# The last matrix products of a fused retention and maxout kernel: two chains change places, and one tile's product is taken by seven products

## The chip, the cores and the metric

The kernel runs on one core of a Trainium2 chip. A core has five engines that work side by side, each on its own queue of instructions in order: TensorE (PE, matrix products into PSUM), VectorE (DVE), ScalarE (ACT), GpSimd (POOL) and SyncE (SP, which here issues the loads and stores). The metric is the device time of one execution in microseconds, the median of several runs.

## The reference

Retention attention gives `x`, and a maxout feed-forward layer with three input matrices and one output matrix follows:

```python
scores = scale * q @ k.T                       # B, H, S, D = 8, 8, 576, 64
ret = scores * where(i >= j, gamma[h] ** (i - j), 0)
x = (ret @ v)                                  # as (4608, 512)
h = maximum(maximum(x @ w1, x @ w2), x @ w3)   # w1..w3: (512, 768)
out = h @ w_out                                # w_out: (768, 512)
```

All is in float32. The weights come as 64-bit floats and are converted in the kernel.

## The kernel before, in words

The 4608 rows are worked in nine tiles of 512 rows (`NT`). For each tile `ffn(t)` computes `h`, held transposed as 6 blocks of 128 features by 512 rows (`h[:, fb, :]`), in three pairs of blocks `fp`, taken in the order 0, 2, 1. Then it multiplies by `w_out`. While a tile runs, the attention of the next tile is put between its products (`steps`, `values`, `scores`).

The first tile's products are plain: `up_plain` and `downs_plain`. From the second tile (`t == 1`) the products of `up` follow a fast scheme with 20 products per block pair (`PRODUCTS`) in chains A to E, each chain a bank in PSUM into which products are added; ACT copies partial sums out (L718, `part`) and DVE joins them (L721). The second tile's down-projection is still `downs_plain` (L745): 6 blocks of `h` times 4 row blocks of 128, 24 matmuls of 512 columns, summed in four banks, then four ACT copies (L749) and four outputs. From the third tile on, `downs` runs 20 products (`DOWNS`, L578), each of two matmuls with 256 columns, in chains C to I. "Place" below is the position in `DOWNS`; `TOTALS` says what is read out after which place, by ACT copy (L567) or DVE sum (L484). The left operands such as `n8` or `b41` are sums of parts of `h` (`HIDDEN_SUMS`), the right ones such as `v13` are sums of parts of `w_out` (`OUT_SUMS`). Two chains share one bank: E with G, H with D, F with C. I has one of its own:

```python
        for pool, tag, chains in ((ps_y, "y", "EG"), (ps_y, "y", "I"), (ps_x, "x", "HD"), (ps_x, "x", "FC")):
...
            begins = chain in "IHEFD" and chain not in begun
```

The pools `ps_x` and `ps_y` have two banks each, handed out in turn, so the next tile's first B chain takes the bank that held H, its first A the bank that held F, its first E the one of E and G. In the profile these banks are called `deg`, `di`, `dhd` and `dfc`; matmuls of `downs` carry their name.

The order on each engine is the order in which the program issues. DVE work that isn't urgent waits in two lists, `urgent` and `chores`; `chore(n)` issues up to `n` of them, and is called between products: after each product of `downs` twice, then one `vraw` scaling on ACT (`scale`, L204). So DVE's queue mixes the totals with the next tile's sums of `x` (`s19`, `s15`, ... L484), transposes (`kT`, `qT`, L209) and masks (L330). `keep_chunk` puts factors on POOL (L340). SP issues loads and outputs in order. Each matmul of float32 appears in the profile as two instructions. `late_room` holds the tiles `late["V"]` and `late["N"]`, which the third tile fills; in the second tile they are not used yet.

Of the kernel before, what the change touches and what calls it, by code (L numbers as in the profile page):

```python
# [40 lines left out]
FP32 = mybir.dt.float32  # L41
# [4 lines left out]
ALU = mybir.AluOpType  # L46
PSUM = bass.MemoryType.PSUM

C = 128
NT = 4 * C  # L50
NH = NT // 2
# [11 lines left out]
            b23 = b43 - b23, n7 = b42 + n4, n5 = b22 + b23, b43 = b41 - b43, b41 = b41 - n5, b23 = b32 + b23,  # L63
            b21 = b21 - b41, b42 = b42 - n5, b22 = b22 - b21, n6 = b31 + n2, b32 = b22 - b32, n8 = b12 - n4,
            b31 = b31 + b32"""
# [15 lines left out]
OUT_SUMS = """m14 = -c21 - c23, m6 = m14 - c13, v19 = c11 - m6, v15 = c12 + v19, v22 = c22 + v15, v3 = v15 + m14,  # L81
              m7 = -c13 - c23, m11 = m7 - c22, v13 = c12 - m11, v10 = c11 + v13, c23 = c22 + c23"""

DOWNS = """I b13 c13, H n1 m14, E b12 c12, H n5 v15, F n7 c22, G n8 c22, E b11 c11, I n2 m6, H b41 v19, I b43 m7,
           H b42 c12, I n4 m11, G n3 c21, I b33 c23, D n6 c21, I b32 v10, C b22 v13, I b23 v3, C b31 c11, I b21 v22"""

TOTALS = {1: "k1 = I", 2: "k14 = H", 4: "k15 = H", 7: "y11 = E + k1", 8: "k6 = I", 9: "k19 = H", 10: "k7 = I",
          11: "y14 = H - k6, k19 = k19 - k6", 12: "k11 = I, k14 = k11 - k14, y24 = F + k14", 13: "y21 = G - k11",
          14: "k20 = I", 15: "y23 = D + k20", 16: "k10 = I, k1 = k1 + k10", 17: "u = C + k7, u = u + k19",
          18: "k3 = I, y12 = u - k3", 19: "k7 = C + k7, y13 = k7 - k1", 20: "y22 = I - k15"}  # L90
X_SUMS, W_SUMS = ([x.split() for x in text.split(",")] for text in (X_SUMS, W_SUMS))
PRODUCTS, DOWNS, OUT_SUMS = ([x.split() for x in text.split(",")] for text in (PRODUCTS, DOWNS, OUT_SUMS))
# [6 lines left out]
def kernel(  # L99
# [14 lines left out]
    nc = tc.nc  # L114
    P = 128
# [29 lines left out]
    def half(j):  # L145
        return slice(D * j, D * (j + 1))
# [55 lines left out]
    def scale(n=1):  # L202
        for _ in range(min(n, len(scaling))):
            scaling.popleft()()  # L204

    def chore(n=1):
        for _ in range(n):
            if urgent or chores:
                (urgent or chores).popleft()()  # L209
# [177 lines left out]
    def head(c, n):  # L387

        return NP * c + n
# [90 lines left out]
            for n, line in enumerate(X_SUMS):  # L480
                soon(partial(step, n, *line))

    def combine(dst, a, b, sign):
        nc.vector.tensor_tensor(dst, a, b, op=ALU.add if sign == "+" else ALU.subtract)  # L484

# [14 lines left out]
    def load_weights(n):  # L502
        for _ in range(n):
            if not to_load:
                return
            i, fb = piece = to_load.popleft()
            if fb % 2 == 0:
                bits[i, fb // 2] = wraw.tile([P, 2, DM], I64, tag="bits", name="bits")
            t = bits[i, fb // 2][:, fb % 2, :]
            if i == "out":  # L510
                nc.sync.dma_start(t, moe_w_out[fb * P:(fb + 1) * P, :])
            else:
                heads = WS[i][:, fb * P:(fb + 1) * P].rearrange("(h p) f -> p h f", p=D)
                blocks = t.rearrange("p (n f) -> p n f", f=P)
                for c in range(2):
                    nc.sync.dma_start(blocks[half(c)], heads[:, head(c, 0):head(c, NP)])

    def groups(order):

# [27 lines left out]
    def downs(t, h, order):  # L547
        n8, n23, n6 = (ppool.tile([P, m, 2, P], FP32, tag="part", name="n") for m in (1, 2, 1))
        late_ones = {"n8": n8[:, 0], "n2": n23[:, 0], "n3": n23[:, 1], "n6": n6[:, 0]}
        for step in sums_of_hidden(h, order, 1, late_ones):  # L550
            step()
        banks = {}
        for pool, tag, chains in ((ps_y, "y", "EG"), (ps_y, "y", "I"), (ps_x, "x", "HD"), (ps_x, "x", "FC")):
            b = pool.tile([P, 2, DM // 2], FP32, tag=tag, name="d" + chains.lower())
            banks.update({chain: b[:, n] for n, chain in enumerate(chains)})
        begun, parts = set(), {}

        def total(dst, _, a, sign=None, b=None):
            a, b = (banks.get(x, parts.get(x)) for x in (a, b))
            if dst[0] == "y":  # L560
                place = opool.tile([P, DM // 2], FP32, tag="osb", name="osb")[:]
            else:
                if dst not in parts:
                    parts[dst] = ppool.tile([P, DM // 2], FP32, tag="part", name=dst)[:]
                place = parts[dst]
            if sign is None:
                nc.scalar.copy(place, a)  # L567
            else:
                combine(place, a, b, sign)
            if dst[0] == "y":  # L570
                i, j = int(dst[1]) - 1, int(dst[2]) - 1
                nc.sync.dma_start(out[t * NT + j * P:t * NT + (j + 1) * P, i * DM // 2:(i + 1) * DM // 2], place)

        for n, (chain, b, v) in enumerate(DOWNS):
            begins = chain in "IHEFD" and chain not in begun
            begun.add(chain)
            for e in range(2):
                nc.tensor.matmul(banks[chain], lhsT=hidden(h, order, b, late_ones)[:, e], rhs=late["V"][v][:, e],  # L578
                                 start=begins and e == 0, stop=chain not in [x[0] for x in DOWNS[n + 1:]] and e == 1,
                                 skip_group_check=True)  # L580
            for line in TOTALS.get(n + 1, ()):
                total(*line)
            yield
# [100 lines left out]
    def weight_sums(fp):  # L684

        def step(dst, a, sign, b):
            combine(*(factor(n, slice(2 * fp, 2 * fp + 2)) for n in (dst, a, b)), sign)

        for dst, _, a, sign, b in W_SUMS:
            chores.append(partial(step, dst, a, sign, b))  # L690
        chores.append(partial(summed_fp.add, fp))
# [98 lines left out]
    def ffn(t):  # L790

        h = hpool.tile([P, NF, NT], FP32, tag="h", name="h")
        if t == 0:
            for fp, i in units:
                if (fp, i) == units[0]:
                    first_ups(h)
                    yield
                    continue
                for fb in (2 * fp, 2 * fp + 1):
                    maximum, = up_plain(t, h, fb, i)  # L800
                    if (fp, i) == units[-1] and fb % 2:
                        maximum()
                        convert(2)
                    else:
                        convert(4 if (fp, i) == units[1] else 2)
                        maximum()
                    if (fp, i, fb) == (*units[1], 0):
                        scores(CPT)
                        state(CPT)
                        keep(CPT)  # L810
                yield
            convert(3)
            for fb, _ in enumerate(downs_plain(t, h, range(NF // 2))):
                convert(2 if fb < 2 else 4 * len(pieces))
                if fb == 2:
                    while_converting.close()
                    late["pool"] = ctx.enter_context(tc.tile_pool(name="late", bufs=1))
                    state_factors()
                    nc.gpsimd.tensor_copy(causal[half(1), 0:D], causal[half(1), half(1)])
                    late_room()  # L820
                    weight_sums(0)
                elif fb == 3:
                    chore(len(chores))
                if fb in (1, 3):
                    yield
            yield
            return
        order = (0, 2, 1)
        if t == 1:
            spread.append(True)  # L830
            weight_sums(2)
            weight_sums(1)
        if t == 2:
            out_sums(order)
        total = len(order) * 2 * len(PRODUCTS)
        count = parts = 0
        for fp in order:
            while fp not in summed_fp:
                chore()
            for step, _ in enumerate(up(t, h, fp)):  # L840
                if step % 4 == 1 or step % 4 == 3 and len(urgent) > (2 if t == 1 else 6):
                    chore(len(urgent) > 0)
                elif chores:
                    chores.popleft()()
                if step % 3 == 2:
                    scale()
                count += 1
                if count * (NF // 2 * 3) >= (parts + 1) * total:
                    parts += 1
                    yield  # L850
            if t > 1 and fp != order[-1]:
                chores.extend(sums_of_hidden(h, order, 3 - order.index(fp)))
        chore(len(urgent) + len(chores))
        if t == 1:
            for n, _ in enumerate(downs_plain(t, h, order)):
                chore(5)
                scale(3)
                if n in (1, 3):
                    yield
        else:  # L860
            for n, _ in enumerate(downs(t, h, order)):
                chore(2)
                scale()
                if n in (3, 9):
                    yield
        yield
# [146 lines left out]
```

## Time and profile before

| | |
|---|---|
| median of 3 runs | 751.48 us (750.33 to 751.66) |
| the profiled execution | 751.75 us, span 749.9 us |
| PE busy | 739.0 us (99%), 6680 instructions |
| DVE busy | 569.6 us (76%), 1040 instructions |
| ACT, POOL busy | 336.2 us (45%), 28.3 us (4%) |
| matmuls of `downs_plain`, L745 | 96 instructions, 42.1 us busy (two tiles) |
| granted clock of PE | 0.999 of full speed |

In the profile a line such as `L745 PE MATMUL down<-w_out,h` is a group: code line, engine, operation, what is written and what is read. In a timeline the first two numbers are the start and the time taken, in us from the span's start, and brackets tell how long the engine stood idle and what released it. PEld is the loading of a matmul's stationary operand, which overlaps other matmuls. Starts are measured; the ends of matmuls are modelled.

### The profile page before, as it was taken

To read this page: it belongs to the slowest core of one execution; us is meant where nothing else is said; L and a number is where in the kernel's file an instruction comes from. 1 tells how busy PE (TensorE), PEld (TensorE's weight loads), DVE (VectorE), ACT (ScalarE), POOL (GpSimd) and SP (SyncE) were. 2 spreads that over 40 slices of the span, in tenths; PEclk is the share of its full clock that TensorE was granted. 3 is DMA by queue.
4 is the path that set the end of the run, shared out by engine and by line. 5 is a ranking of instruction groups with operands and counts; after the bars stand their busy time and mean duration, and the time that the engine had idled before them with its cause. 6 is when DMAs were issued, how large, how long until landed. Compare 5 with 4: busy or idle time off the path is not lost.

```text
span 749.9 us, 16732 instructions
## 1 busy us (share of the span) xinstructions
PE 739.0 (99%) x6680; PEld 600.7 (80%) x6680; DVE 569.6 (76%) x1040; ACT 336.2 (45%) x693; POOL 28.3 (4%) x36
## 2 busy tenths in 40 slices
PE   8999999999999999999999999999999999999998
PEld 6645546887588888888888888888888888888886
DVE  3988899987576895689668876688668956893675
ACT  3764533454245433644254435542455245424441
POOL 2000000001000100000000001000100010000000
PEclk9999999999999999999999999999999999999999
DMA  9996842504152515142433243232514151000001
GB/s 208 239 247 142 225 93 75 96 15 91 47 98 43 98 32 111 38 76 47 100 65 66 49 91 80 46 70 52 114 26 94 39 103 31 1 30 28 1 1 56
DMA packets 229981, 59.30 MB, mean 79 GB/s; under 512 B 211216, under 2 KB 228112, under 8 KB 229904
## 3 DMA queue, kind: packets, MB, share of 16 engines
q1 hardware_dynamic: 228640, 57.98, 35.7%
q8 instruction: 52, 0.85, 0.5%
q10 hardware_dynamic: 1264, 0.27, 0.2%
q14 instruction: 25, 0.20, 0.1%
HBM read 48.76 MB, written 9.44 MB: 78 GB/s over the span
## 4 chain that ended last, share of the span: by engine, by line
PE 78%; DVE 14%; DMA 4%; SPq 2%; issue 1%; ACT 0%; DVEq 0%
PE a L733 18%; PE b L733 16%; PE c L733 9%; PE up L758 6%; PE d L733 6%; PE down L745 6%; PE e L733 6%; PE sk L323 3%; DVE part L721 3%; PE di L578 2%; DVE h L721 2%; DVE s L484 2%; DVE h L484 2%; DMA bits<-in_moe_w_dram 1%; PE dfc L578 1%; PE o L440 1%
## 5 line engine op out<-in xcount | busy, mean ns | idle before, releaser
L721 DVE TENSOR_TENSOR part<-part 128x512 f32<-128x512 f32 x168 | 118.5, 705 | 90.5 <-ACT part L718 87.9
L718 ACT COPY part<-b 128x512 f32<-128x512 f32 x120 | 70.2, 585 | 167.8 <-PE b L733 165.8
L721 DVE TENSOR_TENSOR h<-h,part 128x512 f32<-128x512 f32 x120 | 83.3, 694 | 24.3 <-ACT h L718 19.7
L718 ACT COPY part<-a 128x512 f32<-128x512 f32 x96 | 56.2, 585 | 52.4 <-PE a L733 51.1
L733 PE MATMUL b<-s,n 128*128 128x256 f32 x288 | 73.9, 379 | 0.0
L204 ACT ACTIVATE vraw<-vraw,gk 128x64 f32<-128x64 f32 x208 | 67.5, 347 | 5.4 <-DMA vraw<-in_v_dram 5.4
L758 PE MATMUL up<-xT,w 128*128 128x512 f32 (+2 forms) x160 | 64.2, 554 | 1.0 <-DVE w L627 1.0
L733 PEld LDWEIGHTS b<-s,n 128*128 128x128 f32 x288 | 54.7, 190 | 7.4
L758 PEld LDWEIGHTS up<-xT,w 128*128 128x128 f32 x160 | 28.5, 190 | 31.2 <-issue 26.7
L733 PE MATMUL c<-xT,w 128*128 128x256 f32 x192 | 51.2, 389 | 0.0
L733 PE MATMUL d<-s,w 128*128 128x256 f32 x192 | 49.8, 380 | 0.0
L567 ACT COPY k<-di 128x256 f32<-128x256 f32 x49 | 18.2, 372 | 69.3 <-PE di L578 43.5
L733 PE MATMUL b<-xT,n 128*128 128x256 f32 x192 | 49.3, 379 | 0.0
L733 PE MATMUL a<-s,w 128*128 128x256 f32 x192 | 49.3, 379 | 0.0
L733 PE MATMUL a<-xT,w 128*128 128x256 f32 x192 | 49.3, 379 | 0.0
L733 PE MATMUL a<-xT,n 128*128 128x256 f32 x192 | 45.4, 379 | 0.0
L733 PE MATMUL e<-xT,w 128*128 128x256 f32 x192 | 45.4, 379 | 0.0
L340 POOL TENSOR_TENSOR s<-s,gs_of 64x512 f32<-64x512 f32 x21 | 22.3, 1063 | 532.4 <-DVE s L338 483.9
L745 PE MATMUL down<-w_out,h 128*128 128x512 f32 x96 | 42.1, 594 | 0.0
L733 PEld LDWEIGHTS e<-xT,w 128*128 128x128 f32 x192 | 36.5, 190 | 5.8 <-issue 1.0
L733 PEld LDWEIGHTS a<-xT,n 128*128 128x128 f32 x192 | 36.5, 190 | 5.0
L733 PEld LDWEIGHTS a<-s,w 128*128 128x128 f32 x192 | 36.5, 190 | 5.0
(154 smaller groups left out, 1345.9 us busy)
## 6 DMA issues: line engine op xcount, KB each, us to landing
bits<-in_moe_w_dram SPq DMA_DIRECT2D x36, 256.0 KB, 5.6
kraw<-in_k_dram SPq DMA_DIRECT2D x32, 256.0 KB, 3.2
vraw<-in_v_dram SPq DMA_DIRECT2D x32, 256.0 KB, 3.8
qraw<-in_q_dram SPq DMA_DIRECT2D x224, 32.0 KB, 2.3
kxraw<-in_k_dram SPq DMA_DIRECT2D x224, 32.0 KB, 2.2
out_dram<-osb SPq DMA_DIRECT2D x56, 128.0 KB, 1.7
bits<-in_moe_w_out_dram SPq DMA_DIRECT2D x6, 512.0 KB, 5.7
out_dram<-osb SPq DMA_DIRECT2D x8, 256.0 KB, 2.0
```

Of the source, the lines that this page charges most:

```text
L204: scaling.popleft()()
L323: nc.tensor.matmul(s[half(c), h, :], lhsT=kT[half(c), h, :], rhs=qT[half(c), h, :], start=True, stop=True)
L340: nc.gpsimd.tensor_tensor(new, new, factor, op=ALU.mult)
L440: nc.tensor.matmul(o[m][half(c), n, u, :], lhsT=vds[g][half(m), h, :], rhs=sts[g][half(m), h, :], start=n == 0 and u == 0, stop=place(g, m ...
L484: nc.vector.tensor_tensor(dst, a, b, op=ALU.add if sign == "+" else ALU.subtract)
L567: nc.scalar.copy(place, a)
L578: nc.tensor.matmul(banks[chain], lhsT=hidden(h, order, b, late_ones)[:, e], rhs=late["V"][v][:, e], start=begins and e == 0, stop=chain no ...
L718: nc.scalar.copy(of[step], ps[step[0]][:])
L721: nc.vector.tensor_tensor(of[dst], a, b, op=op)
L733: nc.tensor.matmul(ps[chain][:, e, :], lhsT=factor(w, 2 * fp + e), rhs=xS[t][x], start=n == 1 and e == 0, stop=ends, skip_group_check=True)
L745: nc.tensor.matmul(b[:], lhsT=h[:, fb, m * P:(m + 1) * P], rhs=w_sb["out", fb], start=fb == blocks[0], stop=fb == blocks[-1])
L758: nc.tensor.matmul(ps[:, a:b], lhsT=w_sb[i, fb][:, dc * P:(dc + 1) * P], rhs=xT[t][:, dc, a:b], start=dc == 0 and a == 0, stop=dc == NDC - ...
```

## The change

In `downs`, places 15 and 17 exchange their products (`C b22 v13` comes to 15, `D n6 c21` to 17), places 6 and 7 exchange theirs (`E b11 c11`, `G n8 c22`), and C shares the bank of H, D that of F. The totals follow: `u` is read after place 15, `y23` after place 17.

In the second tile `downs_plain` gives way to `downs_seven`: the 512x768 by 768x512 product is taken as a two by two scheme of seven products (each 256 rows by 3x128 by 256 columns), per block pair. Its left sums `s1` to `s4` are made by `seven_hidden` once per block pair, `s1` and `s2` on DVE, `s3` and `s4` on POOL; its right sums `t1`, `t2`, `t7`, `t4` by `seven_forms`, `t1` and `t2` as chores from the middle of the last block pair, `t7` and `t4` right after the first product. All lie in the tiles of `late["V"]` and `late["N"]`. Three banks are used, one from `ps_x` and two from `ps_y`; three of the copies are partial results that DVE adds to a later product. Between its seven products up to 4 chores and 2 scalings are issued, where before up to 5 and 3 were issued after each of six rounds.

```diff
@@ -81,12 +81,12 @@
 OUT_SUMS = """m14 = -c21 - c23, m6 = m14 - c13, v19 = c11 - m6, v15 = c12 + v19, v22 = c22 + v15, v3 = v15 + m14,
               m7 = -c13 - c23, m11 = m7 - c22, v13 = c12 - m11, v10 = c11 + v13, c23 = c22 + c23"""
 
-DOWNS = """I b13 c13, H n1 m14, E b12 c12, H n5 v15, F n7 c22, G n8 c22, E b11 c11, I n2 m6, H b41 v19, I b43 m7,
-           H b42 c12, I n4 m11, G n3 c21, I b33 c23, D n6 c21, I b32 v10, C b22 v13, I b23 v3, C b31 c11, I b21 v22"""
+DOWNS = """I b13 c13, H n1 m14, E b12 c12, H n5 v15, F n7 c22, E b11 c11, G n8 c22, I n2 m6, H b41 v19, I b43 m7,
+           H b42 c12, I n4 m11, G n3 c21, I b33 c23, C b22 v13, I b32 v10, D n6 c21, I b23 v3, C b31 c11, I b21 v22"""
 
 TOTALS = {1: "k1 = I", 2: "k14 = H", 4: "k15 = H", 7: "y11 = E + k1", 8: "k6 = I", 9: "k19 = H", 10: "k7 = I",
           11: "y14 = H - k6, k19 = k19 - k6", 12: "k11 = I, k14 = k11 - k14, y24 = F + k14", 13: "y21 = G - k11",
-          14: "k20 = I", 15: "y23 = D + k20", 16: "k10 = I, k1 = k1 + k10", 17: "u = C + k7, u = u + k19",
+          14: "k20 = I", 15: "u = C + k7, u = u + k19", 16: "k10 = I, k1 = k1 + k10", 17: "y23 = D + k20",
           18: "k3 = I, y12 = u - k3", 19: "k7 = C + k7, y13 = k7 - k1", 20: "y22 = I - k15"}
 X_SUMS, W_SUMS = ([x.split() for x in text.split(",")] for text in (X_SUMS, W_SUMS))
 PRODUCTS, DOWNS, OUT_SUMS = ([x.split() for x in text.split(",")] for text in (PRODUCTS, DOWNS, OUT_SUMS))
@@ -480,8 +480,8 @@
             for n, line in enumerate(X_SUMS):
                 soon(partial(step, n, *line))
 
-    def combine(dst, a, b, sign):
-        nc.vector.tensor_tensor(dst, a, b, op=ALU.add if sign == "+" else ALU.subtract)
+    def combine(dst, a, b, sign, engine=nc.vector):
+        engine.tensor_tensor(dst, a, b, op=ALU.add if sign == "+" else ALU.subtract)
 
 
 
@@ -515,6 +515,89 @@
                 for c in range(2):
                     nc.sync.dma_start(blocks[half(c)], heads[:, head(c, 0):head(c, NP)])
 
+    def seven_forms(order):
+
+        pieces = [b[:, e, :] for b in late["V"].values() for e in range(2)]
+        pieces += [b.rearrange("p e c -> p (e c)") for b in late["N"].values()]
+        names = [(n, fp) for n in ("t1", "t2", "t4", "t7", "s1", "s2", "s3", "s4") for fp in order]
+        forms = late["S"] = dict(zip(names, pieces, strict=True))
+        for fp in order:
+            for n, (e, i) in {"b11": (0, 0), "b12": (0, 1), "b21": (1, 0), "b22": (1, 1)}.items():
+                forms[n, fp] = w_out[:, fp, e, i * DM // 2:(i + 1) * DM // 2]
+
+        def step(dst, a, b, fp):
+            combine(forms[dst, fp], forms[a, fp], forms[b, fp], "-")
+
+        sums = (("t1", "b12", "b11"), ("t2", "b22", "t1")), (("t7", "b22", "b12"), ("t4", "b21", "t2"))
+        return [[partial(step, *line, fp) for line in group for fp in order] for group in sums]
+
+    def seven_hidden(h, fp):
+        forms = late["S"]
+        for n, (r, e) in {"a11": (0, 0), "a12": (0, 1), "a21": (1, 0), "a22": (1, 1)}.items():
+            forms[n, fp] = h[:, 2 * fp + e, NH * r:NH * (r + 1)]
+
+        def step(dst, a, sign, b, engine=nc.vector):
+            combine(forms[dst, fp], forms[a, fp], forms[b, fp], sign, engine)
+
+        urgent.append(partial(step, "s1", "a21", "+", "a22"))
+        urgent.append(partial(step, "s2", "s1", "-", "a11"))
+        urgent.append(lambda: (step("s3", "a11", "-", "a21", nc.gpsimd), step("s4", "a12", "-", "s2", nc.gpsimd)))
+
+    def downs_seven(t, order):
+
+        forms, banks, kept = late["S"], {}, {}
+        NM = NH // P
+        factors = {1: ("a11", "b11"), 2: ("a12", "b21"), 6: ("s2", "t2"), 7: ("s3", "t7"), 5: ("s1", "t1"),
+                   4: ("a22", "t4"), 3: ("s4", "b22")}
+
+        def keep(b):
+            both = ppool.tile([P, NM, NH], FP32, tag="part", name="part")
+            nc.scalar.copy(both[:], b[:])
+            return both
+
+        def total(r, c, b, other):
+            osb = ppool.tile([P, NM, NH], FP32, tag="part", name="osb")
+            nc.vector.tensor_tensor(osb[:], b[:], other[:], op=ALU.add)
+            block = out[t * NT + r * NH:t * NT + (r + 1) * NH, c * (DM // 2):(c + 1) * (DM // 2)]
+            nc.sync.dma_start(block.rearrange("(m p) d -> p m d", p=P), osb[:])
+
+        def product(n, b, first=False):
+            x, w = factors[n]
+            for fp in order:
+                for m in range(NM):
+                    nc.tensor.matmul(b[:, m, :], lhsT=forms[x, fp][:, m * P:(m + 1) * P], rhs=forms[w, fp],
+                                     start=first and fp == order[0] and m == 0, stop=fp == order[-1],
+                                     skip_group_check=True)
+
+        def bank(pool, tag, name):
+            return pool.tile([P, NM, NH], FP32, tag=tag, name=name)
+
+        x = bank(ps_x, "x", "dx")
+        product(1, x, True)
+        p1 = keep(x)
+        yield
+        y = bank(ps_y, "y", "dy")
+        product(2, y, True)
+        total(0, 0, y, p1)
+        yield
+        product(6, x)
+        u2 = keep(x)
+        yield
+        z = bank(ps_y, "y", "dz")
+        product(7, z, True)
+        p7 = keep(z)
+        yield
+        product(5, x)
+        total(1, 1, x, p7)
+        yield
+        product(4, z)
+        total(1, 0, z, u2)
+        yield
+        product(3, x)
+        osb = keep(x)
+        nc.sync.dma_start(out[t * NT:t * NT + NH, DM // 2:].rearrange("(m p) d -> p m d", p=P), osb[:])
+        yield
+
     def groups(order):
 
         return dict(zip((3, 2, 1), (slice(2 * fp, 2 * fp + 2) for fp in order)))
@@ -550,7 +633,7 @@
         for step in sums_of_hidden(h, order, 1, late_ones):
             step()
         banks = {}
-        for pool, tag, chains in ((ps_y, "y", "EG"), (ps_y, "y", "I"), (ps_x, "x", "HD"), (ps_x, "x", "FC")):
+        for pool, tag, chains in ((ps_y, "y", "EG"), (ps_y, "y", "I"), (ps_x, "x", "HC"), (ps_x, "x", "FD")):
             b = pool.tile([P, 2, DM // 2], FP32, tag=tag, name="d" + chains.lower())
             banks.update({chain: b[:, n] for n, chain in enumerate(chains)})
         begun, parts = set(), {}
@@ -830,6 +913,7 @@
             spread.append(True)
             weight_sums(2)
             weight_sums(1)
+            form_groups = seven_forms(order)
         if t == 2:
             out_sums(order)
         total = len(order) * 2 * len(PRODUCTS)
@@ -844,17 +928,24 @@
                     chores.popleft()()
                 if step % 3 == 2:
                     scale()
+                if t == 1 and fp == order[-1] and step == 19:
+                    chores.extend(form_groups[0])
                 count += 1
                 if count * (NF // 2 * 3) >= (parts + 1) * total:
                     parts += 1
                     yield
-            if t > 1 and fp != order[-1]:
+            if t == 1:
+                seven_hidden(h, fp)
+            elif fp != order[-1]:
                 chores.extend(sums_of_hidden(h, order, 3 - order.index(fp)))
         chore(len(urgent) + len(chores))
         if t == 1:
-            for n, _ in enumerate(downs_plain(t, h, order)):
-                chore(5)
-                scale(3)
+            for n, _ in enumerate(downs_seven(t, order)):
+                if n == 0:
+                    for step in form_groups[1]:
+                        step()
+                chore(4)
+                scale(2)
                 if n in (1, 3):
                     yield
         else:
```

## The prediction

> **What bounds the kernel now.** I begin with the page's first part, then the waits, then the timeline around each wait of TensorE.
>
> ```profile
> PE 739.0 (99%) x6680; PEld 600.7 (80%) x6680; DVE 569.6 (76%) x1040; ACT 336.2 (45%) x693; POOL 28.3 (4%) x36
> ```
>
> TensorE (PE) is busy for 739.0 of 749.9 us. Time therefore comes from fewer matmuls, or from the few gaps between them. The waits, filtered to PE, add up to under 8 us; the two that the change touches are these (total us, times, longest):
>
> ```profile
> PE dfc L578 <- DVE u L484: 2.6, 5, 0.5
> ...
> PE deg L578 <- DVE n L484: 0.5, 1, 0.5
> ```
>
> The first is place 19 of DOWNS, `C b31 c11`: it adds into a bank half that VectorE (DVE) must first read into `u`. PE's timeline of the third tile (start, us, instruction; [idle <- releaser]) shows places 17 to 20:
>
> ```profile
> 279.55 1.03 PE L578 MATMUL dfc<-v,h 128*128 128x256 f32 x4
> 280.41 1.03 PE L578 MATMUL di<-v,h 128*128 128x256 f32 x4
> 281.96 1.13 PE L578 MATMUL dfc<-w_out,h 128*128 128x256 f32 x4 [0.52 <-DVE u L484]
> 282.92 1.03 PE L578 MATMUL di<-v,h 128*128 128x256 f32 x4
> ```
>
> An undisturbed product starts 0.863 us after the one before. From place 18 to place 20 it is 2.51 where 2 x 0.863 = 1.73 is due: the wait costs **0.78 us**, not the 0.52 in brackets, because matmul ends are modelled and the first matmul after a wait also starts without its weights loaded ahead (0.96 to the next start instead of 0.86). Starts are what to measure by. The five occurrences (281.96, 360.69, 439.44, 518.20, 596.96) are alike. DVE in the same stretch:
>
> ```profile
> 279.93 0.39 DVE L484 TENSOR_TENSOR osb<-deg,k 128x256 f32<-128x256 f32 x1
> 280.24 0.69 DVE L209 STREAM_TRANSPOSE qT<-qraw 128x512 f32<-128x512 f32 x1
> 280.85 0.38 DVE L484 TENSOR_TENSOR osb<-dhd,k 128x256 f32<-128x256 f32 x1
> 281.16 0.40 DVE L484 TENSOR_TENSOR k<-k,k 128x256 f32<-128x256 f32 x1
> 281.49 0.41 DVE L484 TENSOR_TENSOR u<-dfc,k 128x256 f32<-128x256 f32 x1
> ```
>
> No gap stands before any of them: DVE is behind with its own queue, and `u` is late because of what lies ahead of it, not because place 17 was late. The read ends at 281.90 and PE goes on 0.06 later. The last tile has the other wait, at place 6:
>
> ```profile
> 732.01 1.03 PE L578 MATMUL dfc<-w_out,hn 128*128 128x256 f32 x4
> 733.50 1.13 PE L578 MATMUL deg<-w_out,n 128*128 128x256 f32 x4 [0.47 <-DVE n L484]
> 734.47 1.03 PE L578 MATMUL deg<-w_out,h 128*128 128x256 f32 x4
> ```
>
> From place 5 to place 7 it takes 2.46 instead of 1.73: **0.73 us**. The second tile's down-projection, in the chain that ended last (start, us, what):
>
> ```profile
> 182.35 6.87 PE down L745 x16
> 189.22 1.09 PE o L440 x64
> 190.31 0.93 PE o L447 x64
> 191.25 13.93 PE down L745 x32
> 205.18 1.73 PE e L733 x8
> ```
>
> It has no gap; it is pure matmul time.
>
> **What the Trainium skill says.** *Perfetto Trace Analysis*, Matmuls, holds larger matmuls more efficient than smaller ones. Here that does not show: 16 instructions of 512 columns take 6.87 us, 0.429 each, and 4 of 256 columns take 0.863, 0.216 each, half to within 1%. *TensorE: Matmul & The Clock Gate*, Step-by-step, has the next weights loaded while a matmul runs; the trace agrees (weight loads start 0.21 us ahead), and a wait loses it, as at 281.96. *GPSIMD Engine Reference*, Key points, says GpSimd contends with two-input VectorE work for SBUF; the trace agrees: a DVE sum usually of 0.70 us took 1.29 while POOL's `s` (1.04 us from 176.67) ran.
>
> **The change, part by part.**
>
> Second tile, PE. Removed: 24 matmuls, two instructions each, 48 x 0.429 = 20.6 us. Added: 7 products x 3 blocks x 2 row blocks = 42 matmuls of 256 columns, 84 x 0.216 = 18.1 us. **Gain 2.5 us**, all on PE's path. (Busy time divided by count gives 0.257 for 256 columns; that counts each run's overlapping tail and is the wrong number here.)
>
> Second tile, DVE and POOL. Added on DVE: 12 sums of `w_out` and 6 of `h`, 128x256, at 0.34 us start to start = 6.1 us, and three 128x512 totals, 2.1 us. Added on POOL: 6 sums; its 128x256 row takes 0.607, so 3.6 us in pairs of 1.2. What hides them:
> - `t1`, `t2` (6 sums) and the second block pair's hidden sums (2) go ahead of the D2 joins. DVE was idle 0.17 + 0.46 + 2.16 us in the third block pair's second half and 0.49 before; 8 x 0.34 = 2.7 fits into that 3.3, plus up to 0.6 of POOL contention.
>
> ```profile
> 180.42 2.15 DVE L721 TENSOR_TENSOR part<-part 128x512 f32<-128x512 f32 x3 [2.16 <-ACT part L718]
> 182.60 0.69 DVE L721 TENSOR_TENSOR h<-h,part 128x512 f32<-128x512 f32 x1
> ```
>
> - That last `h` is what product 1 needs at its fifth matmul, at 182.19 + 4 x 0.43 = 183.9, weights 0.2 earlier; it ends at 183.29. Before, it had 16 us. The slack is 0.4 us, so this is the new tight place: its cost lies between 0 and 1 us; I take 0, since the joins ahead of it are fixed by a ScalarE (ACT) copy, not by DVE.
> - Product 6 needs `s2`, two sums after the last join (186.7), so 187.6; PE arrives at 182.2 + 5.2 + 2.0 = 189.4 and uses that block at 191. `t7`, `t4` end by about 190, product 7 starts at 192. POOL's `s3`, `s4` end by about 189.
> - Totals (1,1) and (1,0) wait for products 5 and 4 (ends near 197.5 and 200.1), and the next tile's `s` sums queue behind them on DVE: they end near 202 instead of 197. The next tile begins at 202.6 and wants `s15` at 204.3 (done by 193) and `s6` at 209.4. Product 3 waits for total (1,1), 198.2, and is due at 199.9. Cost nothing; without that cover at most 1 us once.
> - ACT's three `keep` copies precede product 6, 5 and 4 by a whole product. Its `vraw` scaling that waited for a load until 189.35 now stands behind the second `keep` (192), so it holds nothing up.
> - SP still issues four outputs of 256 KB. The loads behind them left at 206.25 and can leave about 2.5 us earlier. POOL's `s` factors queue behind at most 1.2 us of sums; their reader in PE comes 10 us later.
>
> Tiles 3 to 9, C at 15 and 19. Nothing is added; 20 products stay. In DVE's queue `u` takes the slot of y23's total, right behind `qT`: it starts at 280.85 instead of 281.49 and ends near 281.25, PE free at 281.31. Place 19 is due at 281.28, its weights at 281.07. So the wait shrinks to about 0.03 plus the weight load it uncovers, 0.10: 0.12 us instead of 0.78. **Gain 5 x 0.66 = 3.3 us**; bounds 0 (`u` not earlier) and 3.9 (nothing left). y23's total moves to place 17, where nobody waits for it soon. C at 15 waits for H's reader (ends 277.26, weights due 277.61), D at 17 for F's (279.05, due 279.34): both free. The next tile's B now takes the bank read last at place 19 instead of 15: `k7` ends near 283.2 and B is due at 282.3 + 0.86 + 1.73 = 284.9, so 1.7 us of slack.
>
> Products 6 and 7 swapped. In the last tile E fills place 6 (its inputs are older) and G is due at 732.01 + 1.73 = 733.74, weights 733.53; `n8` ends 733.44. **Gain 0.73 us**, bounds 0.5 and 0.75. `n2` for place 8 (733.78) is due at 734.6: not late. In the other tiles the values' matmuls stand before place 5; nothing changes.
>
> **Sum:** 2.5 + 3.3 + 0.7 = 6.5 us. The profiled execution took 751.75 us (span 749.9, 1.85 outside) and would take 745.2; the median of the runs is 0.27 lower, so **745.0**.
>
> **Rivals.**
> 1. *The second tile's gain goes into new waits* (product 1 for `h`, DVE pushed back by POOL). For: 0.4 us of slack. Against: PE reaches everything else with 1 us or more to spare. All 2.5 lost: 747.5.
> 2. *`u` comes no earlier.* DVE, late by its queue, keeps place 19 waiting: only 2.5 + 0.7, 748.3. Against: `u` moves ahead of two sums. The other end, no wait at all, is 744.4.
> 3. *Slower: the next tile's B waits for `k7`*, at six boundaries. It decides from 1.7 us of DVE delay; each further 0.1 costs 0.6. To eat 6.5 and 1.5 more, `k7` must come 1.7 + 8.0/6 = 3.0 us later: 753.0. Against: DVE's queue holds the same work; only two totals changed places.
> 4. *The small matmuls do not keep 0.216.* At 0.257 the second tile would lose 1.0 instead of gaining 2.5: 748.5. Against: every 256-column run in the trace keeps 0.216.
>
> **How the numbers follow.** Forecast, with place 19 anywhere between a third left and nothing left: 0.80. Rival 1 in good part: 0.09. Rival 2: 0.04. Rival 4: 0.01. Rival 3: 0.03; small effects cancelling: 0.03. A measurement of this kernel tells about 0.2%, 1.5 us, from no change. Faster by more than that: 0.94, same 0.03, slower 0.03. The range runs from 743.8 (nothing left at place 19, and 0.5 of spread) to 747.5 (rival 1 in full).
>
> **What would show it.** Right: place 20 starts 1.73 to 1.9 us after place 18; tile period 78.1 instead of 78.73; no wait of PE on `n` in the last tile; from product 1 to the next tile's E 20.3 us instead of 22.8; no idle DVE-released time before `dx`. Wrong: PE waiting for `u` 0.5 us again, idle before `dx`'s fifth matmul, or before B at a tile's third product.

## The result, and the profile after

| | before | after |
|---|---|---|
| median of 4 runs | 751.20 us (750.33 to 751.66) | 744.94 us (744.22 to 745.97) |
| profiled execution | 751.75 us, span 749.9 us | 744.22 us, span 742.2 us |

The ratio is 0.9919 (95% interval 0.9902 to 0.9936): faster by 0.8%, 6.3 us of the medians, where 745.0 was forecast.

The first part of the page after, for the same engines:

```profile
PE 736.5 (99%) x6716; PEld 608.4 (82%) x6716; DVE 578.3 (78%) x1061; ACT 336.6 (45%) x693; POOL 33.7 (5%) x42
```

PE has 36 instructions more (84 for 48) and is busy 2.5 us less. The waits of PE that the profile still shows are only these, all in the opening of the kernel:

```profile
PE warm L171 <- POOL ident masks.py:199: 1.4, 1, 1.4
PE up L841 <- DVE w L710: 0.5, 1, 0.5
PE qt L287 <- DMA qraw<-in_q_dram: 0.5, 1, 0.5
```

The lines for `u` and for `n` are gone. PE's timeline of the third tile at places 17 to 20, where the banks are now called `dfd` and `dhc`:

```profile
275.88 1.03 PE L661 MATMUL dfd<-w_out,n 128*128 128x256 f32 x4
276.74 1.03 PE L661 MATMUL di<-v,h 128*128 128x256 f32 x4
277.61 1.13 PE L661 MATMUL dhc<-w_out,h 128*128 128x256 f32 x4
278.58 1.03 PE L661 MATMUL di<-v,h 128*128 128x256 f32 x4
```

From place 18 to place 20 it is 1.84 us, before 2.51. No idle time of PE is shown any more, yet place 19 still takes 0.97 to the next start instead of 0.863: its weights were not loaded ahead. The waits filtered to the weight loads (PEld) show the rest:

```profile
PEld dhc L661 <- DVE u L484: 1.3, 5, 0.3
```

The read of `u` that place 19 waits for, in DVE's timeline, stands right behind the transpose `qT`:

```profile
276.56 0.69 DVE L209 STREAM_TRANSPOSE qT<-qraw 128x512 f32<-128x512 f32 x1
277.18 0.38 DVE L484 TENSOR_TENSOR u<-dhc,k 128x256 f32<-128x256 f32 x1
```

In PE's timeline the last tile, places 5 to 7 (F, E, G), with 1.73 us from the first to the third:

```profile
725.04 1.03 PE L661 MATMUL dfd<-w_out,hn 128*128 128x256 f32 x4
725.91 1.03 PE L661 MATMUL deg<-w_out,h 128*128 128x256 f32 x4
726.77 1.03 PE L661 MATMUL deg<-w_out,n 128*128 128x256 f32 x4
```

And the second tile's seven products in PE's timeline. Their banks are `dx`, `dy` and `dz`; the first line is product 1, the last line is the third tile's E:

```profile
181.03 2.75 PE L568 MATMUL dx<-w_out,h 128*128 128x256 f32 x12
183.62 2.75 PE L568 MATMUL dy<-w_out,h 128*128 128x256 f32 x12
...
193.61 2.75 PE L568 MATMUL dx<-m,m 128*128 128x256 f32 x12
196.20 2.75 PE L568 MATMUL dz<-v,h 128*128 128x256 f32 x12
198.79 2.75 PE L568 MATMUL dx<-w_out,hn 128*128 128x256 f32 x12
201.38 1.89 PE L816 MATMUL e<-xT,w 128*128 128x256 f32 x8
```

A product takes 2.59 us from start to start, 12 x 0.216; products 2 and 6, which have the attention's matmuls between them, take about 0.1 more. From the start of `dx` to E ("from `dx` to E" below) it is 20.35 us; before, the down-projection began at 182.19 and E at 205.01, 22.82.

The account of the two profiled executions, by starts:

| | us |
|---|---|
| second tile, 22.82 to 20.35 | 2.47 |
| place 18 to 20 in five tiles, 12.57 to 9.26 in all | 3.31 |
| last tile, place 5 to 7, 2.46 to 1.73 | 0.73 |
| sum | 6.51 |
| the second tile's last products begin at 181.03 instead of 182.19 | 1.16 |
| both spans, 749.9 to 742.2 | 7.7 |

The 1.16 us is not the change's. It is there already at the start of the first tile's down-projection, 98.38 instead of 99.54, which the change leaves as it was; from that start to the second tile's last products it is 82.65 us in every trace of this study. Among these traces the second point lies anywhere between 180.24 and 182.28, depending on the opening stretch, whose waits (such as `up <- w` above) differ from execution to execution. So single spans are compared from that point on below.

### The profile page after: what moved, and what is told of

It is laid out like the page before. It is cut to its first block, busy times and chain, and to the rows that moved or that the text cites. A ratio compares the mean times of both kernels' runs of the same rounds, so it can differ in the third digit from the quotient of the medians.

```text
span 742.2 us, 16834 instructions
## 1 busy us (share of the span) xinstructions
PE 736.5 (99%) x6716; PEld 608.4 (82%) x6716; DVE 578.3 (78%) x1061; ACT 336.6 (45%) x693; POOL 33.7 (5%) x42
## 4 chain that ended last, share of the span: by engine, by line
PE 95%; SPq 2%; DMA 2%; DVE 1%; issue 0%; POOL 0%; DVEq 0%; POOLq 0%
PE a L816 20%; PE b L816 17%; PE c L816 9%; PE di L661 7%; PE up L841 6%; PE d L816 6%; PE e L816 6%; PE dhc L661 5%; PE deg L661 3%; PE sk L323 3%; PE down L828 3%; PE o L440 2%; PE dfd L661 2%; PE o L447 2%; DMA bits<-in_moe_w_dram 2%; PE dx L568 1%
## 5 line engine op out<-in xcount | busy, mean ns | idle before, releaser
L816 PEld LDWEIGHTS a<-xT,w 128*128 128x128 f32 x192 | 36.5, 190 | 5.0
L816 PEld LDWEIGHTS b<-xT,n 128*128 128x128 f32 x192 | 36.5, 190 | 5.0
```

The lines of the kernel that those rows point to most:

```text
L816: nc.tensor.matmul(ps[chain][:, e, :], lhsT=factor(w, 2 * fp + e), rhs=xS[t][x], start=n == 1 and e == 0, stop=ends, skip_group_check=True)
```

## The experiments

The theory: three independent gains on PE's path, each read from starts, 2.5 us of matmul time, 0.66 us at place 19 in each of five tiles, 0.73 us once. Rivals: the second tile's gain comes back as waits, the two parts need each other, the wait on `u` has another cause, or the next tile waits for `k7`. `no_swap`, `k7_late_3`, `join_late` and `s_on_dve` were run once each; of these only the traces are read.

### seven_only: the second tile alone

```diff
-DOWNS, TOTALS and the chains "HC", "FD" of the changed kernel
+DOWNS, TOTALS and the chains "HD", "FC" of the kernel before
```

> The second tile's seven products alone, the tables of the last products as before. My theory: PE's path loses 48 x 0.429 and gains 84 x 0.216, so 2.5 us less than before (751.2): 748.7; from the start of dx to the next tile's E about 20.35 us instead of 22.8; place 18 to place 20 stays at 2.51 in five tiles. Rival (DVE backlog or POOL contention eats it elsewhere): 750 or more, or a start of E more than 20.9 after dx.

Measured: 748.45 us beside 750.86 for the kernel before in the same comparison, ratio 0.9967 (0.9954 to 0.9979), 2.4 us faster. From `dx` to E 20.36 us. In five tiles place 18 to 20 takes 2.49 to 2.56 us, and the old waits stand in the list, here of PE:

```profile
PE dfc L661 <- DVE u L484: 2.6, 5, 0.6
...
PE deg L661 <- DVE n L484: 0.5, 1, 0.5
```

The seven products give their 2.5 us alone, and nothing downstream takes it back.

### places_only: the tables alone

```diff
-DOWNS, TOTALS and the chains "HD", "FC" of the kernel before
+DOWNS, TOTALS and the chains "HC", "FD" of the changed kernel
```

> The tables alone (C at 15 and 19 with H's bank, 6 and 7 swapped), the second tile's down-projection plain as before. My theory: 5 x 0.67 + 0.73 = 4.1 us less than before (751.2): 747.1; place 18 to place 20 takes 1.84 to 1.9. Rival (the two parts help each other, so one alone gives less than its share): above 748.5.

Measured: 747.04 us beside 750.86, ratio 0.9953 (0.9938 to 0.9968), 3.8 us faster; place 18 to 20 takes 1.83 to 1.85 us in all five tiles. Together 2.4 + 3.8 = 6.2 us; the whole change gave 6.3. The parts add up.

### old_banks: the places without the banks

```diff
-for pool, tag, chains in (..., (ps_x, "x", "HC"), (ps_x, "x", "FD")):
+for pool, tag, chains in (..., (ps_x, "x", "HD"), (ps_x, "x", "FC")):
```

> The changed kernel, but C stays with F's bank and D with H's; only the places differ. If a product must wait for a DVE read of the other half of its bank: C at place 15 waits for y24's total, which ends 275.37 where its weights are due at 273.94 (times of the changed kernel's third tile), so a wait of about 1.4 us at place 15 in five tiles, and none at place 19: about 5 x 1.3 = 6 us lost, near 751, and a wait of PE on the DVE osb read of dfc. If only the half counts: no wait at place 15, the same time as the changed kernel, near 745.

Measured: 753.01 us beside 750.86, ratio 1.0023 (1.0015 to 1.0031): slower than the kernel before. Places 14 to 16 of the third tile in PE's timeline:

```profile
272.67 1.03 PE L661 MATMUL di<-w_out,h 128*128 128x256 f32 x4
274.80 1.13 PE L661 MATMUL dfc<-v,h 128*128 128x256 f32 x4 [1.10 <-DVE osb L484]
275.76 1.03 PE L661 MATMUL di<-v,h 128*128 128x256 f32 x4
```

and the DVE sum that releases it, in DVE's timeline:

```profile
274.32 0.42 DVE L484 TENSOR_TENSOR osb<-dfc,k 128x256 f32<-128x256 f32 x1
```

The sum reads F's half of the bank, C writes the other half, and still C waits for it, 2.13 us from start to start instead of 0.86. This program does not wait by half; it waits by bank, or by tile, which the run can't tell apart, as a tile of these pools fills one bank. That agrees with the Trainium skill, *PSUM — Partial Sum Buffer*, PSUM bank collisions raise a hardware error, whose rule is to guard PSUM by bank and group of partitions and not by address; what the chip would do without the wait was not tried. So C could move to 15 without a wait only because H, whose last reader ends two products earlier, took it in. The size was expected too small: the wait came in six tiles, not five (the eighth tile had it too, though its place 19 had never waited). From place 14 to 16 these tiles take 3.09 to 3.23 us instead of 1.73, 8.4 more in all, and their place 19 is now free of any loss, 0.6 less than in the changed kernel. That gives 7.8; from `dx` to the end the trace is 568.9 us (749.3 less 180.41) against 561.2 (742.2 less 181.03), 7.7 more.

### no_swap: places 6 and 7 put back

```diff
-E b11 c11, G n8 c22
+G n8 c22, E b11 c11
```

> The changed kernel with places 6 and 7 put back (G before E). My theory: only the last tile changes, where place 5 to place 7 takes 2.46 us again instead of 1.73 and PE waits 0.5 for DVE's n; 0.7 us in all, too little for the time, to be read in the trace. Rival (the wait has moved or was due to something else): 1.73 stays.

The last tile, places 5 to 7, in PE's timeline:

```profile
726.09 1.03 PE L661 MATMUL dfd<-w_out,hn 128*128 128x256 f32 x4
727.57 1.13 PE L661 MATMUL deg<-w_out,n 128*128 128x256 f32 x4 [0.45 <-DVE n L484]
728.53 0.81 PE L661 MATMUL deg<-w_out,h 128*128 128x256 f32 x3
```

2.44 us instead of 1.73: the swap is worth 0.71 us, in the last tile only (1.83 us in the six others with and without it). The time of this run, 747.02 us, says nothing alone: its second tile's last products began at 182.11, 1.08 later than in the changed kernel's trace.

### u_first: does DVE's queue alone set place 19?

```diff
-                chore(2)
+                chore(0 if n in (12, 13) else 2)
```

(`n` counts the places from 0, so no chore is issued after places 13 and 14.)

> The changed kernel, with no chore issued after places 13 and 14, so that both sums into u stand before the transpose qT in DVE's queue. My theory (u is late only by what lies ahead of it, and the rest at place 19 is an uncovered weight load): u starts near 276.6 instead of 277.18, place 18 to place 20 takes 1.73 instead of 1.84 to 1.9, about 5 x 0.12 = 0.6 us less than the changed kernel, near 744.3. Rival (another release sets place 19): 1.84 stays.

Measured: 744.33 us beside 750.89 for the kernel before, ratio 0.9916 (0.9903 to 0.993). Beside the changed kernel's 0.9919 the times can't tell the two apart; the traces can. DVE's timeline, third tile:

```profile
276.29 0.39 DVE L484 TENSOR_TENSOR osb<-deg,k 128x256 f32<-128x256 f32 x1
276.60 0.41 DVE L484 TENSOR_TENSOR u<-dhc,k 128x256 f32<-128x256 f32 x1
277.04 0.43 DVE L484 TENSOR_TENSOR u<-u,k 128x256 f32<-128x256 f32 x1
277.38 0.70 DVE L209 STREAM_TRANSPOSE qT<-qraw 128x512 f32<-128x512 f32 x1
```

Place 18 to 20 takes 1.72 to 1.73 us in all five tiles, and from `dx` to the end it is 560.6 us instead of 561.2, about 0.6 less. The wait of PEld on `u` is gone. So `u` was late only by its position in DVE's queue, and the remainder at place 19 was the uncovered weight load. By the trace this version is better than the changed kernel by about half a microsecond; the medians, 744.33 and 744.94, are too close to show it.

### k7_late_3 and k7_late_7: the slower rival

```diff
-                combine(place, a, b, sign)
+                for _ in range(3+1 if dst == "y12" else 1):   # 7+1 in k7_late_7
+                    combine(place, a, b, sign)
```

> The changed kernel with the DVE sum for y12 done four times instead of once (the same values), so k7, the last read of C's bank, comes 3 x 0.34 to 0.45 = 1.0 to 1.35 us later in each of seven tiles. My theory: k7 ended 279.35 and the next tile's B wants its weights at 280.96, so 1.55 us are free and B does not wait: places and the start of B as in the changed kernel. Rival (less slack than computed): B starts late.

> The same with the sum for y12 done eight times: k7 comes 2.4 to 3.15 us later. My theory: B, the next tile's third product, waits 0.9 to 1.7 us at each of six boundaries, so the whole is 5 to 10 us slower than the changed kernel, 750 to 755, and the wait is shown before b. Rival (the bank's last read does not hold B, or DVE's delay shows elsewhere): no wait before b.

With three sums more, `k7` ends 281.59 and neither B (282.02) nor A (282.89) is late; from `dx` to the end it is 1.4 us more than in the changed kernel, which the three sums of the last tile account for (3 x 0.45). With seven more, PE's timeline of the next tile's start in k7_late_7:

```profile
280.70 1.89 PE L817 MATMUL e<-xT,w 128*128 128x256 f32 x8
282.43 1.03 PE L817 MATMUL b<-s,n 128*128 128x256 f32 x4
283.89 1.13 PE L817 MATMUL a<-xT,w 128*128 128x256 f32 x4 [0.43 <-DVE k L484]
284.86 1.03 PE L817 MATMUL c<-s,w 128*128 128x256 f32 x4
```

and DVE's:

```profile
279.86 3.64 DVE L484 TENSOR_TENSOR osb<-u,k 128x256 f32<-128x256 f32 x8
283.42 0.42 DVE L484 TENSOR_TENSOR k<-dhc,k 128x256 f32<-128x256 f32 x1
```

B starts on time at 282.43, before `k7` has even begun; A is the one that waits. The bank last read at place 19 goes to A, the fourth product, and not to B, and what stands ahead of the prediction on how the banks are handed out is wrong for this boundary: they do not go simply in turn. A is late by 0.70 us (C at 284.86 instead of 284.16) at five boundaries and by 0.43 at the last, 3.9 us in all. The rest lies at the end: in the last tile the repeated sums stand in the chain that ends last, 7 x 0.45 = 3.2 us. Together that is 7.1 us, as much as the trace is longer from `dx` to the end (568.3 against 561.2); by the medians it is 7.4 (752.32 us, ratio to before 1.002, 1.001 to 1.003). In the changed kernel's third tile `k7` ends 279.35 and A wants its weights at 281.82: the slack is 2.5 us, not 1.7.

### join_late and s_on_dve: the tight place in the second tile

```diff
 # join_late, in after() of up
-            for dst, ins, op in JOINS.get(step, ()):
+            joins = JOINS.get(step, [])
+            if step == "D2" and t == 1 and fp == 1:
+                joins = [joins[0], joins[1], joins[1], joins[2]]
+            for dst, ins, op in joins:
 # s_on_dve, in seven_hidden
-        urgent.append(lambda: (step("s3", "a11", "-", "a21", nc.gpsimd), step("s4", "a12", "-", "s2", nc.gpsimd)))
+        urgent.append(lambda: (step("s3", "a11", "-", "a21"), step("s4", "a12", "-", "s2")))
```

> The changed kernel with one join of D2 (maximum into A3, same values) done twice in the second tile's last block pair, 0.6 to 0.7 us more on DVE ahead of the h that product 1 needs. If, as the changed kernel's trace suggests, nothing was left of the slack (h ends 182.59, weights due 182.55): dx's fifth matmul waits about 0.7 to 0.8 us and the next E comes about 21.1 after the start of dx. If 0.4 us of slack was there, as forecast: about 0.3 and 20.7. If the joins are fixed by the ACT copy: 0 and 20.35.

> The changed kernel with s3 and s4 of the second tile made on DVE instead of POOL: six sums of 0.34 us more on DVE, six of 0.73 to 1.11 us fewer on POOL, so no contention from them. In the changed kernel t7's three sums took 1.62 us beside POOL's s4 where 1.1 is usual. My theory: DVE is as late as before at the joins of D2 (two sums more, 0.7, against the 0.5 that it waited for POOL's s), product 1 waits 0 to 0.3 us for h, product 7 finds s3 ready; dx to the next E 20.35 to 20.65. Rival (POOL took real load off the path): 20.9 or more.

PE's timeline in join_late:

```profile
181.24 1.89 PE L568 MATMUL dx<-w_out,h 128*128 128x256 f32 x8
183.59 1.13 PE L568 MATMUL dx<-w_out,h 128*128 128x256 f32 x4 [0.46 <-DVE h L807]
```

From `dx` to E 21.08 us, 0.73 more than 20.35: the added join cost PE its whole length (four joins took 2.86 us, three 2.13). In s_on_dve it is 20.51, 0.16 more, all of it in product 1 (2.75 to the next start instead of 2.59). PE shows no idle time there; the weight load does:

```profile
182.02 0.73 PEld L568 LDWEIGHTS dx<-w_out,h 128*128 128x128 f32 x4 [0.29 <-DVE h L804]
```

So nothing was left between the `h` and product 1. DVE in the changed kernel:

```profile
176.60 1.61 DVE L484 TENSOR_TENSOR m<-w_out 128x256 f32<-128x256 f32 x2
178.13 0.41 DVE L484 TENSOR_TENSOR m<-w_out,m 128x256 f32<-128x256 f32 x1
178.47 0.68 DVE L804 TENSOR_TENSOR part<-part 128x512 f32<-128x512 f32 x1
179.07 0.74 DVE L484 TENSOR_TENSOR v<-w_out,m 128x256 f32<-128x256 f32 x2
179.74 2.13 DVE L804 TENSOR_TENSOR part<-part 128x512 f32<-128x512 f32 x3
181.90 0.69 DVE L804 TENSOR_TENSOR h<-h,part 128x512 f32<-128x512 f32 x1
```

There is no gap before the joins (179.74), while the ACT copy that they need ended at 179.23: DVE's own queue sets them. The first line is the likely reason: two sums of `w_out` took 1.61 us beside POOL's `s` (1.19 us from 176.74) where two others take 0.74. No run moved POOL's `s`, so this is argued from the overlap. For POOL's `s4` the run s_on_dve shows it: `t7`'s three sums, in the changed kernel and then in s_on_dve:

```profile
187.30 1.62 DVE L484 TENSOR_TENSOR v<-w_out 128x256 f32<-128x256 f32 x3
186.92 1.09 DVE L484 TENSOR_TENSOR v<-w_out 128x256 f32<-128x256 f32 x3
```

In the changed kernel `h` ends 182.59. The fifth matmul (the ninth instruction) is due at 181.03 + 8 x 0.216 = 182.76 and starts on time, but its weight load begins only at 182.65, 0.11 us late.

## Why the prediction was right, point by point

- **What bounds the kernel.** PE, and only its starts tell the price. All three gains came out as start-to-start differences: 2.47, 3.31 and 0.73 against 2.5, 3.3 and 0.73. That the median came within 0.1 us of the forecast (744.94 for 745.0) is partly chance: the four runs lie 1.75 us apart.
- **Second tile on PE.** 0.216 us held for the 256-column matmuls; rival 4 is out.
- **What hides the second tile's DVE work.** Right in effect, wrong in a reason: the step "the joins ahead of it are fixed by a ScalarE copy, not by DVE" failed. They were set by DVE's queue, 0.5 us after the copy, and the slack of 0.4 us came out as nothing (join_late, s_on_dve). The contention term was mis-sized: up to 0.6 us was allowed, 0.87 came (1.61 less 0.74). POOL's six sums were mis-sized too, 5.4 us (33.7 less 28.3) for 3.6, without a cost. Before, the last `h` had about 15 us (183.29 to 198), not 16. That product 1 cost nothing was luck: its weight load was as late as it can be without a loss (see the last section), and each further 0.1 us would have cost as much. What rival 1 begins with, product 1 waiting for `h`, was nearer than the 0.4 us of slack suggests.
- **Product 6 and later, totals (1,1) and (1,0).** As worked out: the totals started at 196.47 and 198.99, the next tile's `s` sums ended near 200.7, and no wait shows.
- **Place 19.** `u` was to start right behind `qT`, with 0.12 us left. It starts at 277.18, ends 277.56, and PE goes on at 277.61; left are 0.11 us in four tiles and 0.18 in one. u_first shows that this remainder is the weight load and goes with the queue position.
- **C with H's bank.** That the places were free was right (place 14 to 16 takes 1.73 us in every tile of the changed kernel); old_banks shows that the pairing of banks is needed, and that without it the same places make the kernel slower.
- **Places 6 and 7.** 0.73 us, shown by no_swap.
- **The next tile's bank.** The step "the next tile's B now takes the bank read last at place 19" failed: A takes it, with 2.5 us of slack. Rival 3's mechanism exists (k7_late_7) but from a later point and at another chain, and the changed kernel stays clear of it.

## What to carry to other kernels

Price a wait from start to start of the instructions around it, not from the idle time shown: 0.52 us shown was 0.78, and losses of 0.1 show no idle time of PE at all. When an engine is late, look whether a gap stands before its instruction; if there is none, its own queue makes it late, so move the needed sum ahead of work that nobody waits for. Before moving a product that accumulates, look who last reads the bank, not only the half, that it goes to.

## What the runs showed of the hardware that was not expected

- A weight load could begin about 0.11 us late without any loss, and what came on top was lost in full. In the changed kernel it began 0.11 us late at product 1's fifth matmul and cost nothing; 0.22 late at place 19 (277.61 for 277.39) cost 0.11. In s_on_dve 0.26 late cost 0.16, in the kernel before 0.89 late at place 19 cost 0.78. Losses of up to 0.2 us of this kind show as no idle time of PE, only of PEld.
- Two-input DVE sums took 0.5 to 0.9 us longer beside one POOL operation: two took 1.61 instead of 0.74 beside POOL's `s`, three took 1.62 beside POOL's `s4` and 1.09 where `s4` was made on DVE itself (s_on_dve).
- The opening stretch varies by 2 us between executions of almost the same program (97.59 to 99.62 at the start of the first tile's down-projection), about as much as the runs of one kernel spread (744.22 to 745.97).
